# LayerNorm of the feed-forward stage in 16 VectorE steps, and block 1's x normalized from head 18 with its transposes two heads apart

## The chip, the cores and the metric

The kernel runs on one NeuronCore of a Trainium2 chip. The metric is the device time of one execution in microseconds (us). The core's engines are called by the profile's names: PE is TensorE (matmuls; PEld are its weight loads), DVE is VectorE, ACT is ScalarE, POOL is GpSimd, SP is SyncE, which here only issues DMAs. Each engine takes its instructions in the order of the program; they meet through semaphores.

## The reference

The inputs are `x` (1 x 2048 x 576), a cache of keys and values for 16 heads (2048 x 128 each, of which the last 512 rows are used), and weights, all bfloat16. Cut to what matters, in plain notation:

```python
x   = A_x
xn  = layernorm(x)
# attention: 32 query heads over 16 cached heads, 512 keys each
q   = (xn @ wq)                       # 32 heads of 128
p   = softmax(q @ k[last 512].T / sqrt(128))
s   = concat(p @ v[last 512]) @ wo
# mixer and feed-forward on the same normalized x
h   = gelu(layernorm(xn) @ w1)        # 576 -> 576
hs  = shift four column groups of h by +1, -1, +2, -2 tokens;  x1 = xn + hs @ w2
h2  = gelu(layernorm(x1) @ w3) @ w4   # 576 -> 4608 -> 576
out = x + s * silu(x1 + h2)
```

There are three LayerNorms: of `x` (called LN1 below), of `xn` (LN2) and of `x1` (LN3). Each needs a mean and a variance for each token, 1/sqrt(variance + eps), and (value - mean) times that.

## The kernel before

**Tiling.** The 2048 tokens are cut into NB = 4 blocks of QB = 512, each of TB = 4 tiles of 128 tokens. A tile has its tokens on the 128 partitions and the 576 columns along the free axis. Matmuls want the transposed form, `xT_b` (5 chunks of 128 columns x 512 tokens; two buffers, used in turn by the blocks). It is made from the normalized tile by a DMA transpose that SP issues, one for each tile of 128 tokens.

**Attention stage.** One long loop goes over U = 4 x 32 units `u`, one head of one block each. The order on PE, SP and POOL is the order written out in that loop (`manual_schedule(engines={SP, POOL, PE})`). The order on DVE and ACT is chosen when the program is built, by a list scheduler with priorities: instructions inside `tc.high_priority` go ahead of others, LayerNorm steps have no such mark. In iteration `u` the loop emits, in this order: the first quarter of the scores of head `u` (`stage_s`, L365), the query projection of head `u+1` (`stage_q`, L350, whose result DVE casts to `qT` at L355 in block 0), the filler steps that were put at `u` with `at` and `later`, then the other score quarters with the two halves of `stage_v(u-1)` in between (L382), and last `stage_t(u-1)`. `stage_v` leaves a PSUM tile `po` of two token tiles; DVE takes the reciprocal of its last column (L386) and multiplies (L387) into the tile `o`. `stage_t` has SP issue one DMA transpose of the finished `o` into `oT` (L395). The pool of `o` has 4 buffers and that of `po` has 2 PSUM banks: L387 of head `u` cannot write before the transpose of head `u-4` has landed, and PE cannot start the next `po` before L387 has read the one two halves earlier.

**LN1 of the next block.** During block `b` the loop also loads and normalizes the `x` of block `b+1`. `ln1_steps` gives nine steps (the functions of `layernorm_steps`): four of statistics (two BN statistics at L133 and an aggregate at L134 each), one of the inverse root (L101 to L110: two preparing operations and three Newton rounds of three operations on 128 x 4 numbers), and four that apply (L144). `later(u1, ..., 3)` puts them three to a head from `u1` on, and `tr1(b+1, tt)` puts the four transposes (L319). For block 0, `u1` is base + 20, and the transposes stand in the fillers of heads 23, 24, 25 and 26. SP takes its queue strictly in order: a transpose whose tile is not yet normalized holds every `oT` transpose behind it. In heads 17 to 21 of block 0 DVE also does the mixer's gelu (L469 to L477) and, at every second head, a copy of transposed keys (L261).

**Loads on POOL.** `load_wo` (L293) and `load_wq` (L227, L229) are issued from POOL at fixed heads; among them, `wo` at head 25, and `wq` at head 27.

**Feed-forward stage.** Here PE, DVE and ACT all run in the written order. Each turn of the loop over `d` does two "ups" (128 hidden features times two each, L731, in 64-row halves that run side by side) and two "downs" (L768). In an up, `first()` fills two PSUM banks from two halves, then `fence` (L721) lets DVE read one element of each bank, and `second()`, which adds the other halves into the same banks, may only start after the fence; likewise between `down(d, 0, .)` and `down(d, 1, .)`. After `second()` DVE copies one bank out (`hx`, L747). Between these, `pop()` takes one step off the list `work` and puts it into DVE's order at that place. The list holds the end of the block before (adds, the four output steps of each tile, L787 to L803) and LN3 of the next block: `ln3_work` hands out the steps of `ln3_steps(b)` one at a time and then the four transposes (L176):

```python
            return [lambda i=i: step(i) for i in range(2 * TB + 1)] + [lambda: ln3_transpose(b)]
```

LN3 of blocks 1, 2 and 3 is done there; LN3 of block 0 is done at the end of the attention stage. In a turn there are six `pop()`s (five in a block's last turn), and a block has nine turns, so 53 places for a block.

Of the kernel before, what the change touches and what calls it, by code (L numbers as in the profile page):

```python
# [8 lines left out]
P = 128  # L9
ACT = mybir.ActivationFunctionType  # L10
ALU = mybir.AluOpType
AX = mybir.AxisListType
BF16 = mybir.dt.bfloat16
FP32 = mybir.dt.float32
I32 = mybir.dt.int32
# [6 lines left out]
LN_EPS = 1e-5  # L22
GELU_A = 0.7978845608028654
GELU_B = 0.7978845608028654 * 0.044715
RSQRT_MAGIC = 1597463007.0
# [6 lines left out]
def kernel(  # L32
# [14 lines left out]
    nc = tc.nc  # L47
# [3 lines left out]
    _, S, D = A_x.shape  # L51
# [12 lines left out]
    TB = QB // P  # L64
    SCALE = float(Dh) ** -0.5
    NF = D // P
    DR = D - NF * P
    NDC = NF + 1
    DP = NDC * P
# [52 lines left out]
    def layernorm_steps(pool, dsts, srcs, rsqrt=rsqrt_newton, twice=False):  # L122
        n = len(srcs)
        hw = D // 2
        st_ = {}

        def stats(i):
            if i == 0:
                st_["mv"] = pool.tile([P, n, 2], FP32, name="ln_mv")
            st = pool.tile([P, 2, 6], FP32, name="ln_st")  # L130
            for j in range(2):
                tc.keep_in_program_order(
                    nc.vector.bn_stats(out=st[:, j, :], in_=srcs[i][:, j * hw:(j + 1) * hw]))  # L133
            nc.vector.bn_aggr(out=st_["mv"][:, i, :], in_=st[:])  # L134

        def inv():
            st_["r"] = rsqrt(pool, st_["mv"][:, :, 1], n)

        def apply(i):
            parts = [(dsts[i], srcs[i])]  # L140
            if twice:
                parts = [(dsts[i][:, 0:D], srcs[i]), (dsts[i][:, D:DP], srcs[i][:, NF * P:D])]
            for dst, src in parts:
                nc.vector.tensor_scalar(out=dst, in0=src, scalar1=st_["mv"][:, i, 0:1],  # L144
                                        scalar2=st_["r"][:, i:i + 1], op0=ALU.subtract, op1=ALU.mult)

        return ([lambda i=i: stats(i) for i in range(n)] + [inv] + [lambda i=i: apply(i) for i in range(n)])

    def layernorm(pool, dsts, srcs):
        for step in layernorm_steps(pool, dsts, srcs):  # L150
            step()
# [7 lines left out]
    small = ctx.enter_context(tc.tile_pool(name="small", bufs=4))  # L159
    x1_t = {}  # L160
# [7 lines left out]

    def ln3_steps(b):
        xm = xm_b[b % 2]  # L170
        return layernorm_steps(small, [xm[:, tt, :] for tt in range(TB)], [x1_t[b][:, tt, :] for tt in range(TB)],
                               twice=True)

    def ln3_transpose(b):
        for tt in range(TB):
            nc.sync.dma_start(out=xT_b[b % 2][:, :, tt * P:(tt + 1) * P], in_=xm_b[b % 2][:, tt, :], transpose=True)  # L176

    with ExitStack() as actx:
# [36 lines left out]
        def load_x(b, eng):  # L215
            x_t[b] = []
            for tt in range(TB):
                xt = xraw.tile([P, D], BF16, name="xt")
                t = b * TB + tt
                eng.dma_start(out=xt[:], in_=x2[t * P:(t + 1) * P, :])  # L220
                x_t[b].append(xt)
# [43 lines left out]
        def late(ap, fn):  # L265
            g = nc.gpsimd.tensor_copy(out=gate[:, :], in_=ap)
            with tc.issue_after(g.ins):
                fn()
# [49 lines left out]
        def transpose_tile(dstT, src, tt):  # L318
            nc.sync.dma_start(out=dstT[:, :, tt * P:(tt + 1) * P], in_=src[:, tt, :], transpose=True)  # L319
# [14 lines left out]
        def tr1(b, tt):  # L334
            transpose_tile(xT_b[b % 2], xn_t[b], tt)
# [64 lines left out]
        def wo_atoms(qb):  # L400
            psp, tag = (ps_pq, "pq") if qb == NB - 1 else (ps_wo, "wo")
            groups = []
            st = {}

            def mm(ps, h, tt, lo, hi):
                nc.tensor.matmul(ps, lhsT=oT_t[qb * Hq + h][:, tt, :], rhs=wo_sb[:, h, lo:hi], start=(h == 0),  # L406
                                 stop=(h == Hq - 1))

            def main(tt, h):
                if tt == 0 and h == 0:  # L410
                    so_t[qb] = so_pool.tile([P, TB, D], BF16, name="s_out")
                if h == 0:
                    st["ps"] = psp.tile([P, M0], FP32, name="pswo", tag=tag)
                mm(st["ps"][:, :], h, tt, 0, M0)
                if h == Hq - 1:
                    nc.scalar.activation(out=so_t[qb][:, tt, 0:M0], in_=st["ps"][:, :], func=ACT.Copy, scale=0.5)

            def rem(tt, h):
                if tt == 0 and h == 0:
                    st["pr"] = psp.tile([P, TB, R0], FP32, name="pswr", tag=tag)  # L420
                mm(st["pr"][:, tt, :], h, tt, M0, D)
                if tt == TB - 1 and h == Hq - 1:
                    nc.scalar.activation(out=so_t[qb][:, :, M0:D], in_=st["pr"][:, :, :], func=ACT.Copy, scale=0.5)
                    (nc.scalar if qb == NB - 1 else nc.sync).dma_start(out=rows(s_dram, qb * TB, TB),
                                                                       in_=so_t.pop(qb)[:])

            for tt in range(TB):
                groups.append([lambda tt=tt, h=h: main(tt, h) for h in range(Hq)])
            groups.append([lambda tt=tt, h=h: rem(tt, h) for tt in range(TB) for h in range(Hq)])
            return groups  # L430
# [4 lines left out]
        def ln2_steps(b):  # L435
            return layernorm_steps(small, [xnn_b[:, tt, 0:D] for tt in range(TB)],
                                   [xn_t[b][:, tt, 0:D] for tt in range(TB)])

        def tr2(b, tt):
            transpose_tile(xnnT, xnn_b, tt)  # L440
# [45 lines left out]
        def b2_shift(b):  # L486
            with tc.high_priority(offset=HP):
                b2_shift_(b)
# [69 lines left out]
        def at(u, fn):  # L558
            fill.setdefault(u, []).append(fn)

        def pe(u, atoms):
            pe_fill.setdefault(u, []).extend(atoms)
# [5 lines left out]
        def later(u, make, per):  # L568
            cell = []
            for i in range(2 * TB + 1):  # L570
                def step(i=i):
                    if not cell:
                        cell.append(make())
                    cell[0][i]()
                at(u + i // per, step)

        for b in range(NB):
            base = b * Hq
            if b > 0:
                for i, group in enumerate(wo_atoms(b - 1)):  # L580
                    pe(base + 1 + i, group)
            later(base + 7, lambda b=b: ln2_steps(b), 3)
            for tt in range(TB):
                at(base + 10 + tt, lambda b=b, tt=tt: tr2(b, tt))
            for c in range(5):
                pe(base + (15 if 0 < b < NB - 1 else 17) + c, b1(b, c))
            for bb in ([b - 1] if b > 0 else []) + ([b] if b == NB - 1 else []):
                o2 = base + (28 if bb == b else 23 if b == NB - 1 else 21)
                at(o2 - 1, lambda bb=bb: b2_shift(bb))
                for tt in range(TB):  # L590
                    pe(o2 + tt, b2(bb, tt))
                pe(o2 + 3, b2_rem(bb))
            if b + 1 < NB:
                at(base + (8 if b == 0 else 4), lambda b=b: late(pT_t[b * Hq + (8 if b == 0 else 4)][0][0:1, 0:1],
                                                                 lambda: load_x(b + 1, nc.gpsimd)))
                u1 = base + (24 if b else 20)
                later(u1, lambda b=b: ln1_steps(b + 1), 3)
                for tt in range(TB):
                    at(u1 + (3 + tt // 2 if b else 3 + tt), lambda b=b, tt=tt: tr1(b + 1, tt))
        for i, group in enumerate(wo_atoms(NB - 1)):  # L600
            pe(U + 1 + i, group)
        at(2, lambda: late(pT_t[2][0][0:1, 0:1], load_w1))
# [21 lines left out]
        with tc.manual_schedule(engines={SP, POOL, PE}):  # L624
# [16 lines left out]
            for u in range(0, max(max(fill), max(pe_fill)) + 1):  # L641
                atoms = pe_fill.get(u, []) + [fn for v, g in pe_late if v == u for fn in prep_k(g)]
                n = len(atoms)
# [18 lines left out]
    with ExitStack() as bctx:  # L662
# [162 lines left out]
        def ln3_work(b):  # L825
            cell = []

            def step(i):
                if not cell:
                    cell.append(ln3_steps(b))  # L830
                cell[0][i]()

            return [lambda i=i: step(i) for i in range(2 * TB + 1)] + [lambda: ln3_transpose(b)]

        def bank_pair(names):
            return [ps_h2.tile([P, QB], FP32, name=n) for n in names]
# [7 lines left out]
        with tc.manual_schedule(engines={PE, DVE, ACTE}):  # L844
# [6 lines left out]
            g, j = 2, 0  # L851
            for d in range(0, ND, 2):
                b = d // NP
# [53 lines left out]
                j = 1 - j  # L907


            b = NB - 1  # L910
# [34 lines left out]
            tt = TB - 1  # L945
# [11 lines left out]
    with tc.If(flag > 0):  # L957
        with ExitStack() as gctx:
# [14 lines left out]
            small = pool("r_small", 4)  # L973
# [4 lines left out]
            with tc.For_i(0, NT, 1) as t:  # L978
# [10 lines left out]
                for h in range(Hq):  # L989
                    g = h // REP  # L990
                    if h % REP == 0:
                        k_nat = work.tile([P, KCH, Dh], BF16, name="r_k")
                        nc.sync.dma_start(out=k_nat[:],
                                          in_=A_k_cache[0, g, K0:, :].rearrange("(kc p) d -> p kc d", p=P))
                        v_g = work.tile([P, KCH, Dh], BF16, name="r_v")
                        nc.sync.dma_start(out=v_g[:],
                                          in_=A_v_cache[0, g, K0:, :].rearrange("(kc p) d -> p kc d", p=P))
# [80 lines left out]
```

## Time and profile before

| | |
|---|---|
| median of 5 runs | 852.92 us (851.38 to 859.62) |
| the profiled execution | 852.8 us, span 851.0 us |
| PE | 832.6 us busy (98%), 7980 matmuls |
| PEld | 486.7 us (57%) |
| DVE | 427.5 us (50%) |
| ACT | 460.9 us (54%) |
| POOL | 76.9 us (9%) |
| HBM | 49.17 MB read, 9.44 MB written |
| attention stage | about 11.7 us (first L350) to 556 us (first L731) of the span |
| feed-forward stage | about 556 us to the end |

The 852.8 us is the whole time of the profiled execution; the 851.0 us is the span from its first to its last instruction. Busy time is the union of an engine's instructions; the idle time before an instruction, and what ended it, stand in square brackets in the timeline. The last matmul of the trace ends at about 843.5 us, and what follows is the last tile's output.

### The profile page before, as it was taken

The page shows a single profiled execution, that of the slowest core. Times are in us where ns is not written, and L with a number is a line of the kernel's source. Part 1 is how long each engine was busy: PE and PEld are TensorE (multiplying, and loading weights), DVE is VectorE, ACT ScalarE, POOL GpSimd, SP SyncE. Part 2 cuts the span into 40 slices and gives each one's busy share as a digit, 9 for nine tenths or more (in the row PEclk, how much of TensorE's full clock was granted, in tenths as well). Part 3 has the DMA queues.
Part 4 walks back from the last instruction along what each step waited for, and adds up shares of the span by engine and source line. Part 5 has one row for each costly group of instructions (what it writes and reads, how often), then busy time and mean ns, then how long its engine had stood idle before and what let it go on. Part 6 is the DMA issues. An engine that isn't in the chain of part 4 may idle for free.

```text
span 851.0 us, 19459 instructions
## 1 busy us (share of the span) xinstructions
PE 832.6 (98%) x7980; PEld 486.7 (57%) x7980; DVE 427.5 (50%) x1351; ACT 460.9 (54%) x825; POOL 76.9 (9%) x134
## 2 busy tenths in 40 slices
PE   8999999999999999999999999999999999999996
PEld 6665555665665566565566565455555555555554
DVE  5788741267751156762154884052247527635333
ACT  4776763498793388784379874132333333334600
POOL 3532200310010111010001100000000000000000
PEclk9999999999999999999999999999999999999998
DMA  6996751364372174363148336993003301310101
GB/s 172 225 249 158 146 107 41 102 129 94 84 140 48 41 130 96 93 124 75 27 82 161 69 83 105 306 327 60 2 2 73 100 2 43 77 55 15 44 18 42
DMA packets 139983, 83.94 MB, mean 99 GB/s; under 512 B 106944, under 2 KB 133248, under 8 KB 139888
## 3 DMA queue, kind: packets, MB, share of 16 engines
q1 hardware_dynamic: 130048, 53.01, 30.7%
q0 software_dynamic: 8448, 28.15, 11.6%
q10 hardware_dynamic: 1392, 1.48, 0.5%
q8 instruction: 64, 1.05, 0.5%
q14 instruction: 31, 0.25, 0.1%
HBM read 49.17 MB, written 9.44 MB: 69 GB/s over the span
## 4 chain that ended last, share of the span: by engine, by line


## 5 line engine op out<-in xcount | busy, mean ns | idle before, releaser
L367 ACT ACTIVATE pT<-sc 128x512 bf16<-128x512 f32 x512 | 290.2, 596 | 104.0 <-PE sc L365 95.9
L365 PE MATMUL sc<-qT,kT 128*128 128x512 bf16 x512 | 182.3, 378 | 0.8 <-DVE qT L355 0.6
L382 PEld LDWEIGHTS <-pT 128*128 128x128 bf16 x2048 | 139.5, 98 | 53.6 <-DVE o L387 3.2
L382 PE MATMUL po<-v_sb,pT 128*128 128x129 bf16 x2048 | 161.4, 220 | 3.0 <-DVE o L387 2.7
L350 PE MATMUL psq<-xT_b,wq_b 128*128 128x512 bf16 x640 | 159.0, 379 | 1.1 <-DMA xT_b<-xn_b 0.8
L386 DVE RECIPROCAL ri_b<-po 128x2 f32<-128x2 f32 x256 | 43.0, 168 | 190.2 <-PE po L382 186.1
L731 PE MATMUL ph<-xT_b,w_s 64*128 64x512 bf16 x976 | 127.1, 376 | 2.3 <-DVE fence L721 2.1
L768 PE MATMUL pm<-w_s,h 64*128 64x512 bf16 x864 | 122.2, 377 | 0.9 <-DVE fence L721 0.9
L406 PE MATMUL pswo<-wo_sb,oT 128*128 128x512 bf16 x512 | 116.7, 379 | 0.0
L387 DVE TENSOR_TENSOR o<-po,ri_b 128x256 bf16<-128x256 f32 x256 | 107.8, 422 | 10.9 <-DMA oT<-o 4.5
L749 ACT ACTIVATE h<-ph 128x512 bf16<-128x512 f32 x67 | 39.4, 597 | 133.9 <-PE ph L731 133.9
L350 PEld LDWEIGHTS <-wq_b 128*128 128x128 bf16 x640 | 62.4, 98 | 74.9 <-issue 2.9
L768 PEld LDWEIGHTS <-h 64*128 64x128 bf16 x1728 | 70.8, 94 | 56.7 <-issue 1.6
L406 PEld LDWEIGHTS <-oT 128*128 128x128 bf16 x1024 | 64.9, 98 | 55.4 <-DMA oT<-o 0.5
L768 PE MATMUL pr<-w_s,h 64*128 64x64 bf16 x864 | 90.2, 189 | 0.2 <-ACT h L749 0.2
L731 PEld LDWEIGHTS <-w_s 64*128 64x128 bf16 x1152 | 57.4, 94 | 50.9 <-issue 2.8
L357 ACT ACTIVATE qT<-psq 128x512 bf16<-128x512 f32 x96 | 57.4, 598 | 28.6 <-PE psq L350 28.6
L747 DVE COPY hx<-ph 128x512 f32<-128x512 f32 x55 | 38.0, 691 | 67.8 <-PE ph L731 67.8
L365 PEld LDWEIGHTS <-kT 128*128 128x128 bf16 x512 | 47.4, 97 | 28.4 <-DVE qT L355 1.2
L227 POOL DMA_DIRECT2D wq_b<-in_A_wq_dram x30 | 23.4, 780 | 315.6 <-PE psq L350 296.2
L721 DVE TENSOR_SCALAR fence<-ph,ph 1x1 f32<-1x1 f32 x61 | 12.6, 206 | 53.1 <-PE ph L731 52.5
L749 ACT ACTIVATE h<-hx 128x512 bf16<-128x512 f32 x55 | 34.6, 630 | 8.5 <-DVE hx L747 7.0
(114 smaller groups left out, 647.3 us busy)
## 6 DMA issues: line engine op xcount, KB each, us to landing
wq_b<-in_A_wq_dram POOLq DMA_DIRECT2D x30, 512.0 KB, 5.5
w_s<-in_B_w_dram SPq DMA_DIRECT2D x9, 576.0 KB, 7.0
wo_sb<-in_A_wo_dram POOLq DMA_DIRECT2D x8, 576.0 KB, 4.9
w_s<-in_B_w_dram SPq DMA_DIRECT2D x9, 512.0 KB, 8.1
x_dram<-x SPq DMA_DIRECT2D x4, 576.0 KB, 3.5
x<-x_dram SPq DMA_DIRECT2D x4, 576.0 KB, 5.1
s_b<-s_dram SPq DMA_DIRECT2D x4, 576.0 KB, 5.6
x_b<-in_A_x_dram SPq DMA_DIRECT2D x4, 576.0 KB, 6.4
```

What stands on the lines that cost most here:

```text
L350: nc.tensor.matmul(psq[:, :], lhsT=w[:, kc, hh * Dh:(hh + 1) * Dh], rhs=xT_b[qb % 2][:, kc, :], start=(kc == 0), stop=(kc == NDC - 1))
L357: nc.scalar.activation(out=qT[:, :], in_=psq[:, :], func=ACT.Copy)
L365: nc.tensor.matmul(sc[:, :], lhsT=kT[:, g, kc * P:(kc + 1) * P], rhs=qT_t[u][:, :], start=True, stop=True)
L367: nc.scalar.activation(out=pT[:, :], in_=sc[:, :], func=ACT.Exp, scale=SCALE)
L382: nc.tensor.matmul(po[:, j, :], lhsT=pTs[kc][:, tt * P:(tt + 1) * P], rhs=v_sb[:, g, kc, 0:Dh + 1], start=(kc == 0), stop=(kc == KCH - 1))
L386: nc.vector.reciprocal(out=ri, in_=po[:, :, Dh])
L387: nc.vector.tensor_tensor(out=o[:, t0:t0 + 2, :], in0=po[:, :, 0:Dh], in1=ri.unsqueeze(2).to_broadcast([P, 2, Dh]), op=ALU.mult)
L406: nc.tensor.matmul(ps, lhsT=oT_t[qb * Hq + h][:, tt, :], rhs=wo_sb[:, h, lo:hi], start=(h == 0), stop=(h == Hq - 1))
L731: nc.tensor.matmul(ps[i][:, :], lhsT=lhsT, rhs=xT[half, kc, :], start=first, stop=last, skip_group_check=True)
L747: nc.vector.tensor_copy(out=src[:, :], in_=ps[i][:, :])
L749: nc.scalar.activation(out=h3[:, :], in_=src[:, :], func=ACT.Gelu_apprx_tanh)
L768: nc.tensor.matmul(out, lhsT=h3_t[b, fc][half, tt * P:(tt + 1) * P], rhs=w4_s[fc // WS][half, fc % WS, lo:hi], start=key not in started, s ...
```

## The change

Three things change. (1) LN3 of blocks 1 to 3 uses a new function, `layernorm_small_steps`, whose steps are smaller: each tile's statistics in two steps (one L133 operation; one L133 operation and the aggregate), the inverse root in four (the two preparing operations; each Newton round), and each tile's apply in one, with the 64 columns of the padded last chunk written before the 576: 8 + 4 + 4 = 16 steps in place of 9, from the same operations. (2) `ln3_work` hands out 3 x TB + 4 = 16 steps. LN3 of block 0 stays as it was. (3) For block 0, `u1` goes from 20 to 18, so LN1 of block 1 is put at heads 18, 19 and 20, and its transposes at heads 21, 23, 25 and 27.

```diff
+    def layernorm_small_steps(pool, dsts, srcs):
+        n = len(srcs)
+        hw = D // 2
+        s = {}
+        mv = pool.tile([P, n, 2], FP32, name="ln_mv")
+        def stats(i, j):
+            if j == 0:
+                s["st"] = pool.tile([P, 2, 6], FP32, name="ln_st")
+            nc.vector.bn_stats(out=s["st"][:, j, :], in_=srcs[i][:, j * hw:(j + 1) * hw])
+            if j == 1:
+                nc.vector.bn_aggr(out=mv[:, i, :], in_=s["st"][:])
+        def begin():
+            s["v"] = pool.tile([P, n], FP32, name="nr_v")
+            nc.vector.tensor_scalar(out=s["v"][:], in0=mv[:, :, 1], scalar1=1.0, scalar2=LN_EPS, op0=ALU.mult,
+                                    op1=ALU.add)
+            s["y"] = pool.tile([P, n], FP32, name="nr_y")
+            nc.vector.tensor_scalar(out=s["y"][:].bitcast(I32), in0=s["v"][:].bitcast(I32), scalar1=-0.5,
+                                    scalar2=RSQRT_MAGIC, op0=ALU.mult, op1=ALU.add)
+        def newton():
+            y = s["y"]
+            t = pool.tile([P, n], FP32, name="nr_t")
+            nc.vector.scalar_tensor_tensor(out=t[:], in0=y[:], scalar=-0.5, in1=y[:], op0=ALU.mult, op1=ALU.mult)
+            nc.vector.tensor_tensor(out=t[:], in0=t[:], in1=s["v"][:], op=ALU.mult)
+            s["y"] = pool.tile([P, n], FP32, name="nr_y")
+            nc.vector.scalar_tensor_tensor(out=s["y"][:], in0=t[:], scalar=1.5, in1=y[:], op0=ALU.add, op1=ALU.mult)
+        def apply(i):
+            for dst, src in [(dsts[i][:, D:DP], srcs[i][:, NF * P:D]), (dsts[i][:, 0:D], srcs[i])]:
+                nc.vector.tensor_scalar(out=dst, in0=src, scalar1=mv[:, i, 0:1], scalar2=s["y"][:, i:i + 1],
+                                        op0=ALU.subtract, op1=ALU.mult)
+        return ([lambda i=i, j=j: stats(i, j) for i in range(n) for j in range(2)] + [begin, newton, newton, newton] +
+                [lambda i=i: apply(i) for i in range(n)])
...
     def ln3_steps(b):
         xm = xm_b[b % 2]
-        return layernorm_steps(small, [xm[:, tt, :] for tt in range(TB)], [x1_t[b][:, tt, :] for tt in range(TB)],
-                               twice=True)
+        dsts, srcs = [xm[:, tt, :] for tt in range(TB)], [x1_t[b][:, tt, :] for tt in range(TB)]
+        return layernorm_small_steps(small, dsts, srcs) if b else layernorm_steps(small, dsts, srcs, twice=True)
...
-                u1 = base + (24 if b else 20)
+                u1 = base + (24 if b else 18)
                 later(u1, lambda b=b: ln1_steps(b + 1), 3)
                 for tt in range(TB):
-                    at(u1 + (3 + tt // 2 if b else 3 + tt), lambda b=b, tt=tt: tr1(b + 1, tt))
+                    at(u1 + 3 + (tt // 2 if b else 2 * tt), lambda b=b, tt=tt: tr1(b + 1, tt))
...
-            return [lambda i=i: step(i) for i in range(2 * TB + 1)] + [lambda: ln3_transpose(b)]
+            return [lambda i=i: step(i) for i in range(3 * TB + 4)] + [lambda: ln3_transpose(b)]
```

## The prediction

> **What bounds the kernel now.** First the page's engine rows, then PE's waits, then the timeline at each wait.
>
> ```profile
> PE 832.6 (98%) x7980; PEld 486.7 (57%) x7980; DVE 427.5 (50%) x1351; ACT 460.9 (54%) x825; POOL 76.9 (9%) x134
> ```
>
> PE is busy 98% of the span. Faster DVE work by itself buys nothing; what the change can win or lose are the few places where PE stands still. PE's waits, longest first:
>
> ```profile
> PE po L382 <- DVE o L387: 2.7, 1, 2.7
> PE ph L731 <- DVE fence L721: 2.1, 2, 1.0
> ...
> PE pm L768 <- DVE fence L721: 0.9, 1, 0.9
> ```
>
> The columns are total us, times, longest. One wait of 2.7 us lies in the attention stage, behind L387; three of 0.9 to 1.0 us lie in the feed-forward stage, behind the fence. The change reaches exactly these four, so I read each. The fence first, DVE's timeline of one of the three (start, length, what):
>
> ```profile
> 568.31 0.16 DVE L101 TENSOR_SCALAR nr_v<-ln_mv 128x4 f32<-128x4 f32 x1
> 568.51 0.17 DVE L103 TENSOR_SCALAR nr_y<-nr_v 128x4 int32<-128x4 int32 x1
> ...
> 570.28 0.16 DVE L110 SCALAR_TENSOR_TENSOR nr_y<-nr_t,nr_y 128x4 f32<-128x4 f32 x1
> 570.36 0.20 DVE L721 TENSOR_SCALAR fence<-pm,pm 1x1 f32<-1x1 f32 x1
> ```
>
> The eleven operations of the inverse root are one step: 568.31 to 570.36, 2.05 us, and the fence is queued behind all of it. PE's timeline has the result: `570.62 ... [0.91 <-DVE fence L721]`. The same happens at 651.75 and 723.74, once for each of LN3's blocks 1 to 3. The other steps are at most 1.06 us long (565.32 to 566.37: a fence and one tile's statistics), and no PE wait stands behind them.
>
> Now the wait in the attention stage: DVE, SP and PE.
>
> ```profile
> 99.14 0.16 DVE L386 RECIPROCAL ri_b<-po 128x2 f32<-128x2 f32 x1
> 99.26 0.43 DVE L144 TENSOR_SCALAR xn_b<-xt,ln_mv,nr_y 128x576 bf16<-128x576 bf16 x1
> ...
> 101.95 0.16 DVE L386 RECIPROCAL ri_b<-po 128x2 f32<-128x2 f32 x1
> 106.60 0.42 DVE L387 TENSOR_TENSOR o<-po,ri_b 128x256 bf16<-128x256 f32 x1 [4.49 <-DMA oT<-o]
> ```
>
> ```profile
> 99.71 1.20 SPq L319 DMA_TRANSPOSE xT_b<-xn_b  x1
> 100.96 1.27 SPq L395 DMA_TRANSPOSE oT<-o  x1
> ```
>
> ```profile
> 98.21 0.63 PE L382 MATMUL po<-v_sb,pT 128*128 128x129 bf16 x8
> ...
> 103.97 0.38 PE L365 MATMUL sc<-qT,kT 128*128 128x512 bf16 x1
> 107.08 0.29 PE L382 MATMUL po<-v_sb,pT 128*128 128x129 bf16 x2 [2.72 <-DVE o L387]
> ```
>
> SP stands at the first transpose of block 1's x (written at head 23, ahead of `oT` of head 22) until the first L144 ends at 99.69, and issues at 99.71. `oT` of head 22 is issued behind it at 100.96. L387 at 106.60 is head 26 (the pool of four `o` holds heads 22 to 25), so it needs just that transfer. The first `po` of head 27 waits for L387: PE idles 2.72 us. The transfer is slow since POOL's loads are in flight:
>
> ```profile
> 96.35 0.79 POOL L293 DMA_DIRECT2D wo_sb<-in_A_wo_dram  x1 [1.15 <-issue]
> 98.26 0.75 POOL L227 DMA_DIRECT2D wq_b<-in_A_wq_dram  x1 [1.12 <-PE psq L350]
> ```
>
> In the tile views of 96 to 108 us, from issue to landing (min/median/max), the transposes into `oT` take 2.5/4.1/5.5 us and those into `xT_b` 2.6/4.9/6.4. The long ones are the first, issued under the loads.
>
> **Part 1, LN3 in 16 steps.** The operations are the same, so DVE's busy time stays. The longest step in front of a fence falls from 2.05 us to three Newton operations (568.71 to 569.30, 0.59 us) or half a tile's statistics with the aggregate (about 0.6 us by 645.81, 646.28 and 646.40). The trace has single steps of 1.06 us ahead of fences without a PE wait, so steps of 0.6 us cost nothing. Gain: the three waits, 0.91 + 1.03 + 1.03 = 2.97 us by PE's rows. By the distance between `hx` copies it is a little more: 567.71 to 572.73 is 5.02, 647.74 to 652.88 is 5.14 and 719.73 to 724.86 is 5.13, against 3.93 in an undisturbed stretch (580.59 to 584.51 and on): 3.5 us. I take -3.3, with -3.6 and -2.0 as ends (a third of it coming back at another fence).
> Costed at nothing: LN3 now fills 17 of the list's places in place of 10. A block's list is 2 adds, 1 load, 17 of LN3 and 16 output steps = 36 of 53 places, so it still drains. The four transposes (L176) are issued 7 places later, about 7/6 of a 7.9 us turn = 9 us, in the fourth of nine turns; block b+1's first up is four turns, over 30 us, off, against landings under 8 us. On SP they are passed by no other issue. If that cover were gone, the wait would be at the first up of a block. The output steps (L787 to L803) only change places with respect to fences, 7 places = one past a whole turn, and they stand at every kind of place today without a wait.
>
> **Part 2, LN1 of block 1 from head 18.** DVE is full here: from 79 to 102 us its timeline shows no idle entry. So the nine steps, asked for two heads sooner, do not all come two heads sooner. In the changed kernel's instruction order the first L144 stands behind the reciprocal (L386) of the first half of head 24; before, behind that of head 25. I count it forward from 95.74, when the last matmul of that `po` of head 24 ends (95.11 + 0.63): L386 at about 95.95; behind it are three Newton operations still to do (0.2 each) and then L144 of 0.4: it ends near 97.1. That is 2.6 us sooner than 99.69. Bounds: 96.5 (DVE a Newton round ahead) and 98.0 (qT and key copies in the way, 0.6 and 0.33).
> The first transpose on SP does move the full two heads: from head 23 to head 21, now ahead of `oT` of head 20. So the L387 that must wait is that of head 24, and the `po` that PE cannot start is the first of head 25, which stands at 98.21 before. Two heads are 6 us of PE time (107.08 - 2.72 - 98.38 = 5.98 between the last matmul before either point); the norm gains 2.6. The hole widens by the difference, 3.4 us, if the transfer takes as long.
> Step by step: L144 ends 97.1; SP issues the x transpose at once (1.2) and `oT` of head 20 at 98.35; landing takes 5.5 us as for its counterpart, 103.9; L387 0.1 later and PE 0.48 later (106.60 to 107.08): 104.5. PE's last matmul before ends at 98.38: idle 6.1 us in place of 2.72, so +3.4. Ends: without the loads 2.5 us to landing gives idle 3.1 (+0.4); landing when it does before, 100.96 + 5.5 = 106.5, gives 107.0, idle 8.7 (+6.0). The loads at 96.35 and 98.26 are issued at the same times in both, as they hang on heads 25 and 27, so the slow end is nearer. Then the spacing of the other three transposes has nothing left to win: all four L144 are done while DVE waits.
> What is queued behind the waiting L387 on DVE: both halves' L387, then reciprocals and `qT`; PE and ACT wait with it, and PE being full, none of it is caught up.
> Small: heads 22 and 23 take about 0.3 us more than their matmuls because DVE trails; statistics moved earlier give perhaps 0.2 back (0 to 0.3): -0.2.
>
> **Clock.** A hole of 6 us may also lower PE's granted clock. The windows view (PE's, DVE's, ACT's, POOL's busy us, then PEclk):
>
> ```profile
> 104.00:107.10 3.10, 0.38 (x3) 0.03 (x2) 0.50 (x2) 0.60 (x1) 0.00 (x0) 1.00 1.42 148
> 843.00:846.30 3.30, 0.46 (x11) 0.31 (x8) 1.77 (x8) 0.28 (x1) 0.00 (x0) 1.00 0.21 73
> 846.30:851.00 4.70, 0.00 (x0) 0.00 (x0) 0.00 (x0) 0.00 (x0) 0.00 (x0) 0.51 0.08 26
> ```
>
> 2.72 us of idle left it at 1.00; after the last matmul (843.46) it fell to half within 3 us. The hole of 6.1 lies beyond both, so I expect a fall. The way back is bounded by the launch: the 28 warm-up matmuls from 7.00 on take 3.19 us (114 ns each, against 58 ns for steady ones of 129 columns, 8 in 0.47), and the pace was full by 11.7, at most 10 us after the first at 1.58. Loss is half of the slow time: 0 to 4.3 us; I take 2.5, from about 5 us at half pace.
> [...] No row of this trace shows a fall inside the loop.
>
> **Sum.** 852.8 (the profiled time) - 3.3 + 3.4 - 0.2 + 2.5 = 855.2. The median, 852.9, is 0.1 above: 855.3.
>
> **Rivals.**
> - *The loads let the transposes through* (not slower). `oT` of head 20 is issued 2.6 us sooner than its counterpart, under `wo` but barely behind `wq`; landing in 2.5 to 3.4 us keeps the hole under 4 us and the clock up. Place: the same L387. Time: 852.9 - 3.3 - 0.2 + 0.4 to 1.2 = 850. It decides once the hole stays below about 5 us with full clock. Against it: the two first transposes under these loads took 6.4 and 5.5 us.
> - *The transfer waits for the loads to end.* Landing at 106.5 as before: hole 8.7, +6.0, clock +3.4: 852.9 - 3.3 - 0.2 + 6.0 + 3.4 = 858.8. For it: the loads are tied to heads, not to the norm.
> - *The small steps do not free the fence.* Another step is behind each; gain 0, attention as forecast: 858.6. Against it: no wait stands behind steps of 1.06 us today.
>
> **How the numbers follow.** Forecast 0.5, loads let through 0.25, transfer waits 0.2, steps do not free 0.05. The likeliest case alone spans 853 to 857.5. The range takes in both neighbours: 849.5 (idle 3.1, no fall, -3.6) to 860.5. About 1% (8.5 us) is what a measurement of this kernel can tell from no change. Every case's centre is inside it; the slow ends (hole 8.7, clock 4.3, gain 2.0) reach 860.9, and something still later would pass 861.4: slower 0.1, same 0.86, faster 0.04.
>
> **What would show it.** Right: PE's waits list no fence waits near 570, 651 and 723 and a `po` wait of about 6 us near 98 to 105 with head 24's L387 behind DMA `oT`; granted clock below 1 after it. Wrong: a `po` wait under 4 us, or fence waits at other steps. A single wait at the first up of a block would refute the cover named above.

## The result, and the profile after

The changed kernel takes 856.14 us in the median of 44 runs, the kernel before 854.98 us in 86 runs beside it (the 852.92 us above are the first five). The ratio is 1.0015, 95% interval 0.9999 to 1.0030: 1.3 us slower, between 0 and 2.6, inside the 1% (8.5 us) that the prediction took for no change. The forecast was 2.4 us slower. Here and below, medians are over all executions, while ratios and intervals leave out the executions in the slow state (more than 1.5% above the same kernel's fastest).

Inside this small difference both parts moved several microseconds, in opposite directions. The page's engine row and PE's waits of the changed kernel (the columns of a wait are total us, times, longest; new lines are 38 further down: L387 is L425, L382 is L420, L319 is L357, L395 is L433):

```profile
PE 833.6 (97%) x7980; PEld 486.3 (57%) x7980; DVE 427.3 (50%) x1351; ACT 461.0 (54%) x825; POOL 76.6 (9%) x134
```

```profile
PE po L420 <- DVE o L425: 10.8, 2, 7.1
PE warm L669 <- POOL ident masks.py:199: 1.6, 1, 1.6
...
PE pr L806 <- ACT h L787: 0.2, 1, 0.2
```

The fence waits are gone (the wait at `warm` is the launch and the same in both kernels), and the `po` wait of 2.7 us has become two, 10.8 us in sum. The longer one is the forecast one. DVE, SP and PE around it, and the time that `oT` of head 20 took to land:

```profile
101.00 0.43 DVE L144 TENSOR_SCALAR xn_b<-xt,ln_mv,nr_y 128x576 bf16<-128x576 bf16 x1
101.35 0.16 DVE L424 RECIPROCAL ri_b<-po 128x2 f32<-128x2 f32 x1
```

```profile
102.77 0.68 DVE L393 CAST qT<-psq 128x512 bf16<-128x512 f32 x1
109.14 0.76 DVE L425 TENSOR_TENSOR o<-po,ri_b 128x256 bf16<-128x256 f32 x2 [5.68 <-DMA oT<-o]
```

```profile
101.46 1.20 SPq L357 DMA_TRANSPOSE xT_b<-xn_b  x1
102.71 2.73 SPq L433 DMA_TRANSPOSE oT<-o  x2
```

```profile
DMA to landing us min/median/max: 6.4/6.4/6.4
```

```profile
102.16 0.38 PE L403 MATMUL sc<-qT,kT 128*128 128x512 bf16 x1
109.61 1.05 PE L420 MATMUL po<-v_sb,pT 128*128 128x129 bf16 x8 [7.08 <-DVE o L425]
```

The first L144 ends at 101.43, and SP, which has stood at that transpose since head 21, issues it at 101.46. `oT` of head 20 goes out behind it at 102.71 and lands 6.4 us later, just ahead of L425 at 109.14. PE has idled since 102.54. All times are about 4 us later than before because of the other wait: 3.8 us near 68 us, with 3.4 us at half clock behind it, a hole that is not the change's (see the last group of experiments).

The windows view shows what the hole does to PE's clock (columns as in the prediction, PEclk, the share of full clock, is the third number from the end):

```profile
102.00:107.10 5.10, 0.54 (x3) 0.04 (x1) 1.45 (x4) 0.63 (x2) 1.28 (x2) 1.00 1.01 253
107.10:110.00 2.90, 0.39 (x4) 0.39 (x5) 0.76 (x2) 0.00 (x0) 0.00 (x0) 0.51 1.20 219
110.00:114.00 4.00, 4.00 (x22) 2.35 (x20) 1.19 (x4) 1.68 (x3) 0.00 (x0) 0.50 0.55 107
114.00:118.00 4.00, 4.00 (x39) 2.58 (x38) 2.54 (x7) 2.40 (x5) 0.00 (x0) 1.00 0.57 80
```

By the trace's clock records the half clock lasts from 107.16 to 113.98, so for 4.4 us after the hole PE works at half pace.

And the feed-forward stage, where a Newton round now stands alone between `hx` and the fence:

```profile
586.56 0.15 DVE L174 SCALAR_TENSOR_TENSOR nr_t<-nr_y 128x4 f32<-128x4 f32 x1
586.75 0.16 DVE L175 TENSOR_TENSOR nr_t<-nr_t,nr_v 128x4 f32<-128x4 f32 x1
586.94 0.16 DVE L177 SCALAR_TENSOR_TENSOR nr_y<-nr_t,nr_y 128x4 f32<-128x4 f32 x1
587.02 0.20 DVE L759 TENSOR_SCALAR fence<-pm,pm 1x1 f32<-1x1 f32 x1
```

**Both traces cut into stages.** Each stage is the distance between two starts on PE in the timeline: the first query matmul of heads 14, 22 and 32 (head 32 is the first of block 1), and the feed-forward stage from its first up to the end of the last matmul.

| us | heads 14 to 22 | heads 22 to 32 | feed-forward | other hole in 14 to 22 | po wait in 22 to 32 |
|---|---|---|---|---|---|
| before | 28.23 | 34.06 | 287.21 | 0 | 2.72 |
| after | 33.83 | 40.14 | 283.23 | 3.76 | 7.08 |

So in these two executions part 2 cost 6.1 us and part 1 gained 4.0, together +2.1; the 5.6 us of heads 14 to 22 is what comes and goes. The whole times of the two executions, 852.8 and 858.4 us, differ by only 5.6, since the changed kernel's first query matmul came 1.2 us sooner and its end after the last matmul was 0.9 us shorter.

### The profile page after: what moved, and what is told of

It is laid out like the page before. It is cut to its first block, busy times and chain, and to the rows that moved or that the text cites. A ratio compares the mean times of both kernels' runs of the same rounds, so it can differ in the third digit from the quotient of the medians.

```text
span 856.6 us, 19444 instructions
## 1 busy us (share of the span) xinstructions
PE 833.6 (97%) x7980; PEld 486.3 (57%) x7980; DVE 427.3 (50%) x1351; ACT 461.0 (54%) x825; POOL 76.6 (9%) x134
## 4 chain that ended last, share of the span: by engine, by line
## 5 line engine op out<-in xcount | busy, mean ns | idle before, releaser
L420 PEld LDWEIGHTS <-pT 128*128 128x128 bf16 x2048 | 140.5, 98 | 62.2 <-DVE o L425 11.8
L420 PE MATMUL po<-v_sb,pT 128*128 128x129 bf16 x2048 | 162.7, 221 | 11.1 <-DVE o L425 10.8
L425 DVE TENSOR_TENSOR o<-po,ri_b 128x256 bf16<-128x256 f32 x256 | 107.7, 421 | 18.2 <-DMA oT<-o 11.8
L395 ACT ACTIVATE qT<-psq 128x512 bf16<-128x512 f32 x96 | 57.4, 598 | 28.6 <-PE psq L388 28.6
L403 PEld LDWEIGHTS <-kT 128*128 128x128 bf16 x512 | 47.6, 98 | 28.2 <-DVE qT L393 0.9
```

Source lines behind the costliest of these rows:

```text
L395: nc.scalar.activation(out=qT[:, :], in_=psq[:, :], func=ACT.Copy)
L403: nc.tensor.matmul(sc[:, :], lhsT=kT[:, g, kc * P:(kc + 1) * P], rhs=qT_t[u][:, :], start=True, stop=True)
L420: nc.tensor.matmul(po[:, j, :], lhsT=pTs[kc][:, tt * P:(tt + 1) * P], rhs=v_sb[:, g, kc, 0:Dh + 1], start=(kc == 0), stop=(kc == KCH - 1))
L425: nc.vector.tensor_tensor(out=o[:, t0:t0 + 2, :], in0=po[:, :, 0:Dh], in1=ri.unsqueeze(2).to_broadcast([P, 2, Dh]), op=ALU.mult)
```

## The experiments

The ratio is always to the kernel before, run beside the experiment. Stages are those of the table above. An edit is shown against the changed kernel, or against the kernel before where the text says so. Each trace is one execution; a single `po` line below is the wait near heads 25 to 27, the other hole not counted. The traces of the fifth `o` buffer and of the norm from heads 18 and 20 with the transposes at 23 and 21 are of executions with a large other hole (45 to 46 us for heads 14 to 22).

### Each part alone

The small steps alone:

```diff
-                u1 = base + (24 if b else 18)
+                u1 = base + (24 if b else 20)
...
-                    at(u1 + 3 + (tt // 2 if b else 2 * tt), lambda b=b, tt=tt: tr1(b + 1, tt))
+                    at(u1 + (3 + tt // 2 if b else 3 + tt), lambda b=b, tt=tt: tr1(b + 1, tt))
```

> Only part 1: LN3 in 16 steps, LN1 and its transposes where they were before (heads 20 and 23 to 26). Theory (SP order): the three fence waits of about 1 us go, the po wait of head 27 stays at about 2.7 us with no clock fall at it; 3.3 us less than before, ratio 0.996. Rival (the small steps only move the wait): fence waits of 2 us or more in sum remain, ratio 1.000.

Measured: ratio 0.9952 (0.9918 to 0.9985), median 848.58 us beside 855.37. The feed-forward stage takes 283.30 us, no fence wait is left, and the `po` wait of head 27 stays:

```profile
PE po L420 <- DVE o L425: 2.8, 1, 2.8
```

One point was missed. Behind this 2.8 us hole the clock did fall (window 113.0 to 116.4, PEclk 0.50):

```profile
113.00:116.40 3.40, 3.40 (x12) 1.40 (x12) 1.57 (x5) 1.39 (x4) 0.00 (x0) 0.50 0.53 105
```

In the trace of before a hole of 2.72 us had left it up (PEclk 1.00). So the hole's size alone does not settle it; what else does, no run shows.

The move to head 18 alone (the kernel before, LN3 in nine steps):

```diff
-                u1 = base + (24 if b else 20)
+                u1 = base + (24 if b else 18)
...
-                    at(u1 + (3 + tt // 2 if b else 3 + tt), lambda b=b, tt=tt: tr1(b + 1, tt))
+                    at(u1 + 3 + (tt // 2 if b else 2 * tt), lambda b=b, tt=tt: tr1(b + 1, tt))
```

> Only part 2: LN1 of block 1 from head 18 and its transposes at heads 21, 23, 25, 27; LN3 in its nine steps as before. Theory (SP order): the po wait lies at head 25 and is 6 to 7 us in place of 2.7, the granted clock falls after it, the three fence waits stay; 4 to 6 us more than before, ratio 1.005 to 1.007. Rival (DVE crowding: the wait comes from the norm's own work standing ahead of L387, and earlier is better): po wait under 2.7 us, ratio below 1.000.

Measured: ratio 1.0053 (1.0021 to 1.0086), median 858.73. Heads 22 to 32 take 38.76 us and the feed-forward stage 287.26, with the fence waits as before. The `po` wait has grown:

```profile
PE po L382 <- DVE o L387: 6.3, 1, 6.3
```

The two ratios, -0.5% and +0.5% with 0.3% either way, add up to the change's +0.15% within their intervals. The rival, that DVE crowding makes the wait, falls.

### Where SP stands

The transposes late, with the norm from head 18:

```diff
-                    at(u1 + 3 + (tt // 2 if b else 2 * tt), lambda b=b, tt=tt: tr1(b + 1, tt))
+                    at(u1 + (3 + tt // 2 if b else 7 + tt), lambda b=b, tt=tt: tr1(b + 1, tt))
```

> The changed kernel with LN1 of block 1 still from head 18, but its transposes at heads 25, 26, 27 and 28. Theory (SP order): the norm ends near head 25 or 26, so SP never stands at an x transpose for more than a microsecond; no po wait over 0.5 us near heads 24 to 28, no clock fall there, no fence waits: 6 us less than before, ratio 0.993. Rival (DVE crowding): nothing changes on DVE's load, so a po wait of several us stays, ratio 1.00. Rival (POOL's loads slow the oT transfers by themselves): the oT transfers near 98 to 106 us still land 5 us after issue and a po wait of 1 us or more stays.

Measured: ratio 0.9898 (0.9853 to 0.9944), median 847.27. Heads 22 to 32 take 30.82 us, and no `po` wait behind L425 is left. SP still issues the first x transpose when L144 ends (96.12), but stands at it for under two microseconds (94.4 to 96.2), not for fifteen (86.4 to 101.5 in the changed kernel):

```profile
93.15 1.19 SPq L433 DMA_TRANSPOSE oT<-o  x1
96.15 1.20 SPq L357 DMA_TRANSPOSE xT_b<-xn_b  x1
97.47 1.21 SPq L433 DMA_TRANSPOSE oT<-o  x1
```

The rival that POOL's loads make the wait by themselves falls too: they slow the transfers just as much here (the `oT` issued at 97.47 took 8.3 us to land, the second x transpose 8.1), and PE waited for none of them.

The kernel before with nothing changed but the place of its transposes:

```diff
-                    at(u1 + (3 + tt // 2 if b else 3 + tt), lambda b=b, tt=tt: tr1(b + 1, tt))
+                    at(u1 + (3 + tt // 2 if b else 6 + tt), lambda b=b, tt=tt: tr1(b + 1, tt))
```

> The kernel before with nothing changed but the four x transposes, at heads 26, 27, 28 and 29 in place of 23 to 26; LN1 from head 20, LN3 in nine steps. Theory (SP order): the po wait of 2.7 us at head 27 goes, the three fence waits stay: 2.9 us less than before, ratio 0.9966. Rival (DVE crowding, or the norm is simply too late): the wait stays at 2.7 us or moves to the query projection of head 32 as a wait on xT_b; ratio 1.000 or above.

Measured: ratio 0.9921 (0.9885 to 0.9956), median 849.07. The stage shows what was expected, 31.20 us in place of 34.06 (-2.9), and no wait of head 27. The ratio says more, 3.8 to 9.8 us; a clock fall spared, as behind the 2.8 us hole above, would be up to an estimated 1.9 us of it (the loss there), and the rest is not explained by the one trace. The 31.20 us are also what this stage takes undisturbed with the norm at head 20; with the norm at head 18 it is 30.8.

The norm from head 18, the transposes back at heads 23 to 26 (`5 + tt` in that line):

> The changed kernel with the norm from head 18 but the x transposes at the old heads 23, 24, 25 and 26. Theory (SP order): the norm is 2 to 3 us sooner than before and SP's place is the old one, so the wait of head 27 shrinks from 2.7 us to 0 to 1 us, no clock fall there: 6 us less than before, ratio 0.992 to 0.994. Rival (the norm's place decides, not the transposes'): as the changed kernel, a wait of 6 to 7 us; ratio 1.0015.

Measured: ratio 0.9939 (0.9900 to 0.9978). The wait is 1.3 us, a little over what was expected, against 2.8 us with the norm at head 20 (the small steps alone). So asking for the norm sooner helps where SP's place stays, as far as one trace of each can tell:

```profile
PE po L420 <- DVE o L425: 1.3, 1, 1.3
```

The norm from head 20 with the transposes at heads 21, 23, 25 and 27:

> The changed kernel with the norm back at head 20 but the x transposes at the new heads 21, 23, 25 and 27. Theory (SP order): the widest hole of all, since SP stands two heads sooner for a norm that is not asked for sooner; po wait at head 25 of 7 to 10 us, two windows of half clock: 2 to 4 us more than the changed kernel, ratio to before 1.004 to 1.007. Rival (the norm's place decides): as the kernel with the small steps alone, 0.995.

Measured: ratio 1.0044 (1.0006 to 1.0082), a wait of 7.0 us, and 39.71 us for heads 22 to 32, not more than the changed kernel's 40.14:

```profile
PE po L420 <- DVE o L425: 7.0, 1, 7.0
```

The place of the transposes decides, but the two norms cannot be told apart here. The first L144 ends 0.3 us after PE's last matmul here and 1.1 us before it in the changed kernel, yet the hole is the same. The traces point to a reason, though no run tried it alone: in both POOL issues the `wq` load 0.1 us before PE stops, and `oT` of head 20 lands 0.9 and 0.2 us after the last piece of that load. Then the end of the hole hangs on that load, and a norm that ends sooner buys nothing.

### The o buffers and the loads

One more buffer for `o`:

```diff
-        o_pool = pool("o_pool", 4)
+        o_pool = pool("o_pool", 5)
...
-        oT_pool = pool("oT_pool", 36)
+        oT_pool = pool("oT_pool", 35)
```

> The changed kernel with five buffers for o in place of four (and 35 in place of 36 for oT, to make the room). Theory (SP order through the o buffers): the L387 that has to wait is one head later, so the po wait shrinks by one head of PE time, 2.9 to 3.1 us, from 7.1 to about 4 us, with one clock fall left: 3 to 5 us less than the changed kernel, ratio to before 0.996 to 0.998. Rival (POOL's loads alone set when the transfers land, whichever buffer waits): the wait keeps its length; ratio 1.0015.

Measured: ratio 0.9962 (0.9916 to 1.0008). The wait is 4.7 us, 2.4 less than in the changed kernel, where one head's 2.9 to 3.1 had been expected: the hole is counted in `o` buffers.

```profile
PE po L420 <- DVE o L425: 4.7, 1, 4.7
```

POOL's last `wo` load five heads later (`4 + 3 * i + 5 * (i == 7)` for its head):

> The changed kernel with POOL's last load of wo at head 30 in place of 25, so that only the wq load is in flight when SP issues the held transposes. Theory (the held oT needs 5 to 6 us because loads are ahead of it): oT of head 20 lands 1 to 3 us sooner and the po wait is 4 to 6 us; ratio to before 0.998 to 1.000. Rival (the transposes are slow by themselves, two in a row): landing and wait as in the changed kernel, 6 to 7 us; ratio 1.0015 to 1.003.

Measured: ratio 0.9960 (0.9916 to 1.0003), lower than expected but with an interval that holds 0.998; the wait is 4.8 us:

```profile
PE po L420 <- DVE o L425: 4.8, 1, 4.8
```

The first x transpose, with no load ahead of it, now lands 2.6 us after issue (4.3 in the changed kernel). So this one load is a third of the hole. The rest is not SP's queue alone: the `wq` load is still in flight, and `oT` takes 4.1 us to land against 2.4 alone; without that too the hole would be an estimated 3.1 us (4.8 - 1.7). A run without the `wq` load was not made.

### The other hole, and the change without it

Heads 14 to 22 take 28.2 us in some traces and up to 46 in others, also of kernels whose order is the same up to head 21 (28.3 with the transposes late, 33.8 in the changed kernel, 45.0 with the transposes back at head 23). In a slice of it, 52 to 68 us, the DMA view has for the `wo` loads and the `oT` transposes (count, KB each for the loads, median us from issue to landing), in the changed kernel and then in the kernel before:

```profile
wo_sb<-in_A_wo_dram POOLq DMA_DIRECT2D x2, 576.0 KB, 11.5
...
oT<-o SPq DMA_TRANSPOSE x5, 11.9
```

```profile
wo_sb<-in_A_wo_dram POOLq DMA_DIRECT2D x2, 576.0 KB, 6.4
...
oT<-o SPq DMA_TRANSPOSE x6, 6.3
```

Loads and transposes are both nearly twice as slow where the hole is. Four `o` buffers are four heads, some 12 us (an estimate from the 5.98 us of two heads in the trace of before), so at 12 us PE waits. The last four runs move two loads from heads 13 and 16 to heads 18 and 20, out of this slice:

```diff
-        for i in range(8):
-            at(4 + 3 * i, lambda i=i: late(pT_t[4 + 3 * i][0][0:1, 0:1], lambda: load_wo(i)))
+        for i, u in enumerate((4, 7, 10, 18, 20, 19, 22, 25)):
+            at(u, lambda i=i, u=u: late(pT_t[u][0][0:1, 0:1], lambda: load_wo(i)))
```

On the kernel before:

> The kernel before with nothing changed but the two loads of wo, at heads 18 and 20 in place of 13 and 16. Theory (loads under LN2's transposes make the hole at heads 14 to 20): no po wait near 60 to 80 us; times from 849.5 to 853 us with the holes of head 27 and of the fences left; ratio 0.994 to 0.997. Rival (another cause): spread and median as before, 1.000.

Measured: ratio 0.9966 (0.9943 to 0.9989), median 850.40 (849.59 to 854.0), against 849.82 to 868.64 for the kernel before beside it. Heads 14 to 22 take 28.34 us, `oT` lands after 4.9 us in that slice.

```profile
oT<-o SPq DMA_TRANSPOSE x7, 4.9
```

On the changed kernel:

> The changed kernel with the same two loads of wo at heads 18 and 20. It measures the change without the other hole: against the kernel before with the shifted loads. Theory (the sum on record, with the clock falling in every run): po wait of 6 to 7 us at head 25 with half clock after it, no other hole; 1 to 3 us above the kernel before with shifted loads. Rival (the change is neutral, what was measured is the spread): equal to it within 0.5 us.

Measured: ratio 0.9984 (0.9961 to 1.0006), median 852.59: 2.2 us above the 850.40 of the kernel before with the same shift; by the ratios it is 1.5 us. One hole is left, of 6.9 us in place of 2.1:

```profile
PE po L420 <- DVE o L425: 6.9, 1, 6.9
```

This is the change with most of the disturbance taken out, and it agrees with the forecast's 2.4. One of the twelve executions still took 864.57 us; no profile shows which stage lost the time.

The transposes one head apart, at 21, 22, 23 and 24 (`3 + tt`):

> The changed kernel with the shifted loads and the x transposes one head apart (21, 22, 23, 24) in place of two. Theory (only the first transpose's place sets the hole, since all four tiles are normalized while DVE waits): the same hole within 0.7 us and the same time within 1 us as with two heads apart. Rival (the spacing is what helps oT through): a second po wait or a hole 1.2 us or more longer, 2 us or more above.

Measured: ratio 0.9979 (0.9955 to 1.0003), median 852.05 against 852.59 with two heads apart, a difference inside the noise, and a hole of 6.2 in place of 6.9 us. The spacing buys nothing.

Last, the version that the experiments point to: small steps, norm from head 18, transposes at heads 25 to 28, and the shifted loads:

> LN3 in 16 steps, LN1 of block 1 from head 18, its transposes at heads 25 to 28, and POOL's fourth and fifth loads of wo at heads 18 and 20 in place of 13 and 16. Theory (a second hole, at heads 14 to 20, comes and goes between executions, where loads on POOL delay the transposes of LN2's output and the oT behind them): neither hole is left, the times lie within 2 us of each other, 843 us; ratio to before 0.984 to 0.988. Rival (that hole has another cause): times still spread over 10 us, ratio as without the shift of the loads, 0.990.

Measured: ratio 0.9877 (0.9843 to 0.9911), median 843.40, and its six times lie between 843.16 and 844.04. It beats both kernels. In its trace no wait of PE stands behind L425 or a fence; heads 14 to 22 take 28.23, heads 22 to 32 take 30.81 and the feed-forward stage 283.61 us. Of the ten traces without the shifted loads eight have a stretch of heads 14 to 22 that is 1.6 to 18 us longer, of the four with them none.

## Why the prediction was right, step by step

- **Part 1** was -3.3 and is -4.0: every kernel with nine steps has 287.2 or 287.3 us there, every one with sixteen 283.2 to 283.7. The mechanism held; the term was sized from the three distances between `hx` copies (3.5) and shaded down. Besides these waits, the 0.2 us of `PE ph L731 <- DVE hx L747` of before is gone in the changed kernel; four kernels with sixteen steps still have it, and they are the ones at 283.6 or 283.7. Nothing came back at another fence, and the later transposes (L176) met no wait.
- **Part 2, the hole**: forecast 6.1 us with 3.1 and 8.7 as ends; 7.1 in the profiled execution, 6.3, 6.9 and 6.2 in the other three with that order. The path is the forecast one: SP's standstill, `oT` of head 20, the L387 of head 24, the first `po` of head 25. The norm's end relative to PE's last matmul was right within 0.2 us (1.3 forecast, 102.54 - 101.43 = 1.1 measured). The landing was short: 5.5 taken, 6.4 measured. `oT` of head 20 landed at 109.11, 0.2 us after the last piece of the `wq` load, and in the other three traces with that order also 0.2 to 0.3 us after it. So the rival in which the transfer waits for the loads to end had a real share of it. In time the forecast was nearer: with the move to head 18 alone, where PE stops at 98.43 (98.38 forecast), `oT` landed at 104.27, against 103.9 forecast and 106.5 in the rival.
- **The clock**: forecast 2.5. Taking the undisturbed 30.81 us and the hole from the stage leaves 40.14 - 30.81 - 7.08 = 2.25; in the three others, computed the same way, 1.6 to 2.9. What is not sure is the other side of that term, that the kernel before pays nothing: its profiled execution did not (34.06 - 31.20 - 2.72 = 0.1, with the undisturbed stage of the norm at head 20), but the small steps alone lost 35.87 - 31.20 - 2.78 = 1.9 us behind an equal hole. No run shows the 3.4 us that one rival puts on the clock, nor the slow end of 4.3: the four holes above, of 6.2 to 7.1 us, cost 1.6 to 2.9.
- **The norm two heads sooner was credited with 2.6 us** of the hole. With the transposes at head 21 the experiments cannot tell the two norms apart (7.0 and 7.1 us); with the transposes at head 23 it is worth about 1.5 (2.8 to 1.3). This share of the forecast's reasoning is not supported where the change puts the transposes.
- **The spacing has nothing left to win**: so it was.
- **The small term**, the norm's earlier start in the undisturbed heads, was -0.2 and is 30.81 - 31.20 = -0.4.
- **The sum** is nearer than its terms: in the profiled pair they were off by -0.7 (part 1), +1.0 (the hole), -0.4 (the clock, both sides) and -0.2 (the small term), which leaves +2.1 of the forecast's +2.4. That much of the closeness is errors that cancel.
- **Not foreseen**: the other hole. It makes 5.6 us between the two profiled executions, as much as their whole times differ, and reading these two traces alone would have put it on the change.

## What to carry to other kernels

When a DMA on an in-order queue waits for compute, ask what stands behind it, not what it needs itself: pulling the request forward without the data only lengthens the queue's standstill (here to fifteen us at one transpose), and the price is counted in the buffers of whoever stands behind (here 7.1 us with four `o` buffers, 4.7 with five). Move the issue to where the data is surely ready, and check that its reader still has slack (here the transposes could go four heads later with no new wait of PE). And before a single pair of profiles is read as cause and effect, cut both into stages and see whether a stage that the change does not touch has moved.

## What the runs showed of the hardware

- The granted clock stood at half for 3.4 us behind the 2.8 us hole of the small steps alone (113.0 to 116.4, PEclk 0.50), for 3.4 us behind the 3.8 us hole of the changed kernel (69.61 to 73.02) and for 6.8 at its 7.1 us hole (107.16 to 113.98). In it with the shifted loads, where the 6.9 us hole was the only one, the mean granted clock was 0.991, against 0.993 with both holes. A hole's price did not follow from its size alone: the 2.72 us hole of before cost 0.1 us with PEclk at 1.00, the 2.78 us hole of the small steps alone cost 1.9. In the kernel before with late transposes, where PE's longest waits were 2.6 us at the launch and 2.4 us, the mean granted clock was 0.993, against 0.997 in the trace of before. What decides between a hole that costs nothing and one that does, these runs do not show.
- In these traces the transposes on SP's queue slowed down far more than POOL's loads when both were in flight. A transpose into `oT` took 2.4 us from issue to landing when alone, and transposes took 4 to 8 under one or two POOL loads; in the changed kernel a `wo` and a `wq` load took 4.4 and 5.3 us with no transpose in flight (issued at 90.7 and 91.4), and 4.7 and 6.0 with them (100.5 and 102.4). From 105.5 to 107.5 us there the transposes' queue moved 161 packets beside 130 of the loads, and 1674 in the 2 us after that, beside 18 of the loads. In one execution (the norm at head 20 with early transposes) the four transposes of LN2's output took 7.3 to 18.5 us. What makes the same instructions land in 6.3 us in one execution (the median of `oT` from 52 to 68 us before) and in 11.9 in the next (the changed kernel) was not tried and stays open; with two loads moved, all four traces had heads 14 to 22 undisturbed (28.2 to 28.3 us in the two given above).
